# A spectral filter beside a gated MLP on one core: one complex edge column, half-array blocks of four, and the forward constant loaded later

## The chip, the core and the metric

The kernel runs on one core of a Trainium2 chip. The metric is device time in microseconds for one execution. A core has TensorE (matrix products into PSUM, eight banks of 512 fp32 columns per partition), VectorE (DVE), ScalarE (ACT), GpSimd (POOL) and SyncE (SP). SP, ACT and POOL issue transfers, which run on 16 DMA engines. In the profile PE stands for TensorE's products and PEld for its weight loads.

## What is computed

For x of 2048 x 512 (bf16):

```
g = sigmoid(sum(x * gate_w, -1))
a = irfft2(rfft2(x) * (w_r + 1j*w_i))          # 2048 x 257 filter
b = (h * tanh(softplus(h))) @ w2,  h = x @ w1 + b1     # 512 -> 1792 -> 512
out = g * a + (1 - g) * b
```

Branch a is a chain of small Fourier products, branch b two dense products. They share TensorE.

## The kernel before

**Branch b.** `f_mm1` (L790) makes h for four row tiles (512 columns) and one of 14 feature tiles, four products of 512 columns to a group; there are four chunks of 14 groups. `mish` on ACT (L799) moves it from two PSUM banks into one of three activation buffers. `f_mm2` (L831) multiplies 14 feature tiles by w2 into one 512-column bank for each of 16 row tiles, in two halves of seven products; L813 is the last tile in two column halves. Two banks (4 and 5) take mm2's results in turn. For the first NBF = 8 tiles, `evict_b` (L770) stores (1 - g) b without waiting for branch a, and `sum` (L849) adds g a later. For the others, `fin` (L841, and L820 for the last tile) combines both straight from PSUM and so needs branch a's tile first.

**Branch a, forward.** `f_tr` (L517) transposes each x tile, VectorE forms sums and differences (L532), and `f_a1` (L546 to L549) makes the transform along the 512 columns with the constant FDs: bank 0, evicted (`e1`) to In1. With 256 real and 256 imaginary columns wanted for 257 frequencies, the sine column of frequency 0, which would be zero, holds frequency 256. `f_s1` (L569, L571) is the first step along the 2048 rows. It works on half the array: the contraction is 64 deep, and two tiles' products on the upper and the lower half run at the same time. Its real input is 257 columns wide, its imaginary one 255. It takes two row tiles at a time into banks 4 to 7; `e2` evicts to Y1, and a DMA for every four tiles and half (`r1w`) writes scr1 in DRAM in pieces of 257 bf16 columns, 514 bytes. Once all is written, four DMAs (`r1r`) read it back rearranged into In2.

**Filter.** `f_s2` (L680), the second step along the rows, also uses half the array (64 output rows to a product), two units of 256 columns at a time into banks 0 and 1. VectorE multiplies each unit by the filter twice (`wm`, L691), POOL or VectorE combine (`wz`, L697) into Zb, which has three buffers of two units. Columns 0 and 256 go a way of their own: `f_s2x` (L648) for each half of the units, four small VectorE products (`zq`), four on POOL (`zr`, `zi`, `z0r`, `z0i`), a copy `wc` (L701) into Zb's first column. `f_s2i` (L711) inverts the step, half the array again, into banks 6 and 7; `e4` (1024 columns, L446 or L447) evicts, and `r2w` writes scr2, four units to a DMA in pieces of 2 KB.

**Branch a, back.** When scr2 is complete, eight `r2r` read it; then for each of the 16 tiles `f_s1i` (L744), an eviction, `f_a1i` (L756), the gated eviction `geo` on ACT (L761), and two halves of `ga` (L764). The gate's dot products `gdot` (L591) run on VectorE after the last s1; `gcol` and `omg` make g and 1 - g.

**Order.** A planner in the file (`_Graph.schedule`, L221) orders all work when the kernel is built. It gives each task a duration and a priority, takes of the tasks that can start within 0.1 us of the earliest the one of highest priority, and writes a fixed order for each engine, with semaphore waits. It does not see the chip: if a transfer is later than L293 to L297 assume, the engine's queue waits in that order. L293 to L297 put the end of a transfer at

```
xs = max(est + t.dur + 1.0, dq_free)
dq_free = xs + t.xfer
t.done = dq_free + 0.6 + 0.4 * (est > 12.0)
```

with `t.xfer` the bytes over a rate of 300 KB per us unless another is given. TensorE's branch-a work has priority, and mm1 and mm2 fill what is free; 40 warming products on zeros (L504) are dropped once the first mm1 is placed. All loads but a few go through SP in the order of the code from L475: x tile 0, x tiles 1 to 3, w1's first piece (feature tiles 0 and 1), w1's second, x tiles 4 to 7 and so on. FDs is issued on ACT's queue at the start. The wide loads of the filter and of w2 are issued by POOL.

Of the kernel before, what the change touches and what calls it, by code (L numbers as in the profile page):

```python
# [16 lines left out]
KR = 257  # L17
# [298 lines left out]
NBF = 8  # L316
# [4 lines left out]
def _build(nc, A_x, A_w_r, A_w_i, B_x, B_w1, B_b1, B_w2, gate_w, out):  # L321
# [9 lines left out]
    G = _Graph()  # L331
    es = ExitStack()
    with es:
# [14 lines left out]
        misc = sb("misc", [128, 5632], F32)  # L348
        WT = sb("WT", [128, 2, 16, KR], BF)
# [15 lines left out]
        weff = sb("weff", [128, 2, 2, 16], F32)  # L365
        q1 = sb("q1", [128, 2, 2, 16], F32)
# [8 lines left out]
        gEO = misc[:, 2048:3072].rearrange("p (b n) -> p b n", b=2)  # L375
        Zb = miscb[:, 6144:9216].rearrange("p (b u c n) -> p b u c n", b=3, u=2, c=2)
        TT = miscb[:, 9216:11264].rearrange("p (b j n) -> p b j n", b=4, j=4)
# [99 lines left out]
        dma("ld_fd", FDs[:], d_FD[:], writes=["FD"], nbytes=128 * 1536, queue="act")  # L477
        dma("ld_b1", braw[:, :], B_b1.rearrange("(ft p) -> ft p", p=128), writes=["braw"], nbytes=3584, queue="pool")
        ld_w1(0)
        ld_w1(1)  # L480
# [22 lines left out]
        for i in range(NWARM):  # L503
            G.add(f"warm{i}", "pe", 0.213, lambda e: e.matmul(ps[:, 7, 0:256], zt[:, 0:128], zt[:, :], start=True, stop=True),  # L504
               reads=["zt"], prio=1.0).filler = True
# [5 lines left out]
        for t in range(NT):  # L511
            tbk = 3 + t if 1 <= t < 4 else 1
# [30 lines left out]
        for t in range(NT):  # L543
# [15 lines left out]
            if t % 2 == 1:  # L559
                def f_s1(e, t0=t - 1):  # L560
                    ins = None
                    for tt_ in range(2):
                        tk = t0 + tt_
                        for c in range(2):
                            for bx in range(2):
                                r = slice(64 * bx, 64 * bx + 64)
                                o = ps[:, 4 + 2 * tt_ + bx, :]
                                if c == 0:
                                    ins = e.matmul(o[:, 0:KR], M1s[r, tk, 0, :], In1[r, tk, 0:KR], start=True, stop=False)  # L569
                                else:  # L570
                                    ins = e.matmul(o[:, 1:256], M1s[r, tk, 1, :], In1[r, tk, KR:512], start=False, stop=True)  # L571
                    return ins

                B47 = [("bank", i) for i in range(4, 8)]
                s1_tasks.append(pe(f"s1_{t}", 4 * mm(256) + 0.19, f_s1, reads=[("In1", t - 1), ("In1", t), ("m1", t // 8)], writes=B47, prio=SP0 + 0.4))
                yo = Y1.rearrange("p (b t) k -> p t b k", b=2)
                for i in range(2):
                    evict(f"e2_{t - 1 + i}", 514, yo[:, t - 1 + i], ps[:, 4 + 2 * i:6 + 2 * i, 0:KR],
                          [("bank", 4 + 2 * i), ("bank", 5 + 2 * i)], [("Y1", t - 1 + i)], prio=SP0 + 0.6)
            if t % 4 == 3:  # L580
                for bx in range(2):
                    b0 = 16 * bx + t - 3
                    t_r1w.append(dma(f"r1w{t}_{bx}", scr1_w[:, b0:b0 + 4, :], Y1[:, b0:b0 + 4, :],
                                     reads=[("Y1", t - i) for i in range(4)], writes=[("scr1", b0 + i) for i in range(4)],
                                     nbytes=128 * 4 * 514, prio=SP0 + 1.0))
# [3 lines left out]
        for t in range(NT):  # L589
# [3 lines left out]
                  reads=[("x", t), "gw"], writes=[("gd", t), "junk"], deps=s1_tasks[-1:])  # L593
# [9 lines left out]
        def f_wcols(e):  # L603
            ins = None
            for i in range(2):
                e.tensor_copy(out=wrv[:, i, :, 0], in_=WT[:, i, 0, 0:KR:256])
                e.tensor_copy(out=wrv[:, i, :, 1:16].rearrange("p k g -> p g k"), in_=WT[:, i, 15:0:-1, 0:KR:256])
                ins = e.tensor_scalar(out=wh[:, i, :].rearrange("p (k g) -> p g k", k=2), in0=WT[:, i, :, 0:KR:256],
                                      scalar1=0.5, scalar2=None, op0=ALU.mult)
            return ins  # L610

        G.add("wcols", "pool", 1.9, f_wcols, reads=WALL, writes=["wrv", "wh"])
        psW = ps[:, 5, 64:128]
# [7 lines left out]
        def f_weff(e):  # L621
            e.scalar_tensor_tensor(out=weff[:, 0].rearrange("p k g -> p (k g)"), in0=psW[:, 0:32], scalar=0.5, in1=wh[:, 0, :], op0=ALU.mult, op1=ALU.add)
            return e.scalar_tensor_tensor(out=weff[:, 1].rearrange("p k g -> p (k g)"), in0=psW[:, 32:64], scalar=-0.5, in1=wh[:, 1, :], op0=ALU.mult, op1=ALU.add)
# [5 lines left out]
        for hf in range(2):  # L629
            for h in range(2):  # L630
# [3 lines left out]
                                 deps=s1_tasks[-1:], nbytes=128 * 8 * 514, prio=SP0 + 1.0))  # L634
# [6 lines left out]
        for hf in range(2):  # L641
            gs = slice(8 * hf, 8 * hf + 8)

            def f_s2x(e, hf=hf):
                ins = None
                for c in range(2):
                    for h in range(2):
                        ins = e.matmul(ps[64 * h:64 * h + 64, 6, 16 * c:16 * c + 16].rearrange("p (k g) -> p k g", k=2), RF[:, c, :],  # L648
                                       In2[:, 16 * h + 8 * hf:16 * h + 8 * hf + 8, 0:KR:256].rearrange("p g k -> p k g"),
                                       start=True, stop=True)  # L650
                return ins

            s2_tasks.append(pe(f"s2x{hf}", 0.15, f_s2x, reads=[("In2", 16 * h + 8 * hf + i) for h in range(2) for i in range(8)] + ["sm"],
                               writes=[("bank", 6)]))
            xps = ps[:, 6, 0:32].rearrange("p (c k g) -> p c k g", c=2, k=2)

            def f_q(e, gs=gs, xps=xps):
                ins = None
                for c in range(2):
                    e.tensor_tensor(out=q1[:, c, :, gs], in0=xps[:, c], in1=weff[:, c, :, gs], op=ALU.mult)  # L660
                    ins = e.tensor_tensor(out=q2[:, c, :, gs], in0=xps[:, c], in1=weff[:, 1 - c, :, gs], op=ALU.mult)
                return ins

            G.add(f"zq{hf}", "dve", 0.6, f_q, reads=[("bank", 6), "weff"], writes=[("q", hf)])
            G.add(f"zr{hf}", "pool", 0.15, lambda e, gs=gs: e.tensor_tensor(out=zr[:, :, gs], in0=q1[:, 0, :, gs], in1=q1[:, 1, :, gs], op=ALU.subtract),
                  reads=[("q", hf)], writes=[("zr", hf)])
            G.add(f"zi{hf}", "pool", 0.15, lambda e, gs=gs: e.tensor_tensor(out=zi[:, :, gs], in0=q2[:, 0, :, gs], in1=q2[:, 1, :, gs], op=ALU.add),
                  reads=[("q", hf)], writes=[("zi", hf)])
            G.add(f"z0r{hf}", "pool", 0.15, lambda e, gs=gs: e.tensor_tensor(out=z0[:, 0, gs], in0=zr[:, 0, gs], in1=zi[:, 1, gs], op=ALU.subtract),
                  reads=[("zr", hf), ("zi", hf)], writes=[("z0r", hf)])  # L670
            G.add(f"z0i{hf}", "pool", 0.15, lambda e, gs=gs: e.tensor_tensor(out=z0[:, 1, gs], in0=zi[:, 0, gs], in1=zr[:, 1, gs], op=ALU.add),
# [289 lines left out]
```

## Time and profile before

| | |
|---|---|
| median of 3 runs | 144.88 us (144.8 to 145.26) |
| profiled execution | 145.94 us, span 143.9 us |
| TensorE busy | 136.0 us, 95% of the span |
| VectorE / ACT / POOL busy | 85.2 / 82.4 / 34.3 us |
| L790 (mm1), 224 products | 52.1 us busy for the 215 recorded |
| L831 (mm2), 210 products | 47.7 us busy for the 202 recorded |
| granted TensorE clock | 1.0 throughout |

A busy product of 512 columns has 379 ns in the list of groups because products overlap; in a row without gaps they follow each other every 213 ns (256 columns: 107 ns). The span runs from the first to the last instruction. The first L790 starts at 8.11 us, the last s1 at 41.61, the first s2 at 54.77, the last s2i at 92.49, the first s1i at 102.85, and the last a1i ends at 125.66; from there to 140.8 TensorE has only mm2 to do.

### The profile page before, as it was taken

The page shows a single profiled execution, that of the slowest core. Times are in us where ns is not written, and L with a number is a line of the kernel's source. Part 1 is how long each engine was busy: PE and PEld are TensorE (multiplying, and loading weights), DVE is VectorE, ACT ScalarE, POOL GpSimd, SP SyncE. Part 2 cuts the span into 40 slices and gives each one's busy share as a digit, 9 for nine tenths or more (in the row PEclk, how much of TensorE's full clock was granted, in tenths as well). Part 3 has the DMA queues.
Part 4 walks back from the last instruction along what each step waited for, and adds up shares of the span by engine and source line. Part 5 has one row for each costly group of instructions (what it writes and reads, how often), then busy time and mean ns, then how long its engine had stood idle before and what let it go on. Part 6 is the DMA issues. An engine that isn't in the chain of part 4 may idle for free.

```text
span 143.9 us, 2505 instructions
## 1 busy us (share of the span) xinstructions
PE 136.0 (95%) x928; PEld 72.4 (50%) x945; DVE 85.2 (59%) x188; ACT 82.4 (57%) x126; POOL 34.3 (24%) x69
## 2 busy tenths in 40 slices
PE   6879999999999997999999999999999999999991
PEld 4636556555544324344443544443567666644470
DVE  0256777843349996778755866500169999844141
ACT  4437998877775673791448666557557765610000
POOL 4000370030000004346418431200044365420000
PEclk9999999999999999999999999999999999999999
DMA  4899999999975396700303003035953333202032
GB/s 130 288 375 387 383 241 222 227 331 324 147 86 150 64 258 268 280 14 0 146 5 146 2 5 146 0 146 171 271 145 73 75 91 81 52 0 55 18 91 57
DMA packets 16556, 21.40 MB, mean 149 GB/s; under 512 B 1248, under 2 KB 12384, under 8 KB 16160
## 3 DMA queue, kind: packets, MB, share of 16 engines
q1 hardware_dynamic: 15408, 17.03, 42.0%
q0 software_dynamic: 832, 3.94, 10.4%
q10 hardware_dynamic: 304, 0.26, 0.8%
q8 instruction: 7, 0.11, 0.3%
q14 instruction: 5, 0.04, 0.1%
HBM read 14.93 MB, written 6.30 MB: 148 GB/s over the span
## 4 chain that ended last, share of the span: by engine, by line
PE 84%; DMA 10%; DVE 2%; issue 1%; SPq 1%
PE ps L831 30%; PE ps L790 27%; PE ps L756 5%; DMA Abuf<-scr 4%; DMA scr<-Ybuf 3%; PE ps L680 3%; PE ps L711 3%; PE ps L517 3%; PE ps L744 2%; PE ps L549 2%; PE ps L813 2%; DMA xo<-in_A_x_dram 2%; PE ps L569 2%; PE ps L571 1%; PE ps L546 1%
## 5 line engine op out<-in xcount | busy, mean ns | idle before, releaser
L790 PE MATMUL ps<-xT,w_sb 128*128 128x512 bf16 x215 | 52.1, 379 | 1.9 <-DVE yb L532 1.1
L799 ACT ACTIVATE act<-ps,b1f 128x512 bf16<-128x512 f32 x56 | 38.4, 687 | 17.6 <-PE ps L790 17.2
L831 PE MATMUL ps<-w_sb,act 128*128 128x512 bf16 x202 | 47.7, 379 | 0.4
L790 PEld LDWEIGHTS ps<-xT,w_sb 128*128 128x128 bf16 x224 | 19.9, 98 | 24.5 <-ACT act L799 4.4
L831 PEld LDWEIGHTS ps<-w_sb,act 128*128 128x128 bf16 x210 | 20.0, 98 | 22.4 <-issue 0.4
L691 DVE TENSOR_TENSOR misc<-ps,WT 128x512 f32<-128x512 f32 x32 | 19.9, 682 | 9.4 <-PE ps L680 9.4
L764 POOL TENSOR_TENSOR Tg<-misc 128x256 bf16<-128x256 f32 x14 | 11.1, 810 | 25.0 <-ACT misc L761 25.0
L697 POOL TENSOR_TENSOR misc<-misc 128x255 bf16<-128x255 f32 x19 | 13.4, 729 | 14.1 <-DVE misc L691 14.1
L447 ACT ACTIVATE Ybuf<-ps 128x514 bf16<-128x514 f32 (+1 forms) x16 | 12.5, 784 | 4.6 <-PE ps L711 4.3
L761 ACT ACTIVATE misc<-ps,gcol 128x512 f32<-128x512 f32 x16 | 10.6, 687 | 7.1 <-PE ps L756 7.1
L446 DVE CAST misc<-ps 128x512 bf16<-128x512 f32 x8 | 5.5, 681 | 13.4 <-PE ps L744 13.4
L764 DVE TENSOR_TENSOR Tg<-misc 128x256 bf16<-128x256 f32 x18 | 12.8, 747 | 0.4 <-ACT misc L761 0.4
L770 ACT ACTIVATE xo<-ps,omg 128x512 bf16<-128x512 f32 x8 | 5.5, 687 | 10.7 <-PE ps L831 7.1
L591 DVE SCALAR_TENSOR_TENSOR junk<-xo,gwb 128x512 bf16<-128x512 bf16 x16 | 11.0, 690 | 0.7
L841 DVE SCALAR_TENSOR_TENSOR xo<-ps,omg,Tg 128x512 bf16<-128x512 f32 x7 | 5.1, 745 | 7.9 <-PE ps L831 7.9
L756 PE MATMUL ps<-GDs,misc 128*128 128x256 bf16 x64 | 9.4, 273 | 0.0
L446 DVE COPY xT<-ps 128x512 bf16<-128x512 bf16 x9 | 3.8, 424 | 9.3 <-PE ps L517 9.2
L446 DVE CAST Abuf<-ps 128x512 bf16<-128x512 f32 x6 | 4.1, 690 | 7.1 <-PE ps L549 7.1
L446 DVE CAST Ybuf<-ps 128x514 bf16<-128x514 f32 (+1 forms) x8 | 6.1, 756 | 2.9 <-PE ps L571 2.9
L756 PEld LDWEIGHTS ps<-GDs,misc 128*128 128x128 bf16 x64 | 6.0, 98 | 2.3
L517 PE MATMUL ps<-pid,xo 128*128 128x128 bf16 x64 | 6.1, 225 | 0.2 <-DMA xo<-in_A_x_dram 0.2
L680 PE MATMUL ps<-Abuf,sm 128*64 128x256 bf16 x64 | 5.1, 278 | 1.2 <-DMA Abuf<-scr 1.1
(69 smaller groups left out, 123.9 us busy)
## 6 DMA issues: line engine op xcount, KB each, us to landing
scr<-Ybuf SPq DMA_DIRECT2D x8, 257.0 KB, 11.0
Abuf<-scr SPq DMA_DIRECT2D x4, 514.0 KB, 6.3
scr<-Ybuf SPq DMA_DIRECT2D x4, 512.0 KB, 3.0
Abuf<-scr SPq DMA_DIRECT2D x8, 256.0 KB, 5.3
w_sb<-in_B_w_dram POOLq DMA_DIRECT2D x2, 896.0 KB, 16.0
out_dram<-xo SPq DMA_DIRECT2D x14, 128.0 KB, 2.3
w_sb<-in_B_w_dram SPq DMA_DIRECT2D x3, 512.0 KB, 9.1
xo<-in_A_x_dram SPq DMA_DIRECT2D x3, 512.0 KB, 9.7
```

Of the source, the lines that this page charges most:

```text
L446: G.add_multi(name, [("dve", dve_dur(n), lambda e: e.tensor_copy(out=dst, in_=src)), ("act", act_dur(n), lambda e: e.activation(dst, src, ...
L447: ("act", act_dur(n), lambda e: e.activation(dst, src, AF.Copy))],
L517: ins = e.transpose(psb[:, tbk, 128 * dt_:128 * (dt_ + 1)], xo[:, t, 128 * dt_:128 * (dt_ + 1)], perm[:, :])
L591: lambda e, t=t: e.scalar_tensor_tensor(out=junk[:, :], in0=xo[:, t, :], scalar=1.0, in1=gwb[:, :], op0=ALU.mult, op1=ALU.mult, accum_out= ...
L691: lambda e, Pb=Pb, Wu=Wu, u=u, pb=pb: e.tensor_tensor(out=Pb[:, pb, :].rearrange("p (c r q) -> p c r q", c=2, r=4), in0=ps[:, u % 2, :].re ...
L697: fz = (lambda e, c=c, Pb=Pb, op=op, pb=pb, zb=zb: e.tensor_tensor(out=Zb[:, zb, pb, c, 1:256], in0=Pb[:, pb, 1:256], in1=Pb[:, pb, 257:51 ...
L756: ins = e.matmul(ps[:, yk, 256 * (j // 2):256 * (j // 2) + 256], TT[:, ts_, j, :], GDs[:, j, :], start=(j % 2 == 0), stop=(j % 2 == 1))
L761: lambda e, t=t, gb=gb, yk=yk: e.activation(gEO[:, gb, :], ps[:, yk, :], AF.Copy, scale=gcol[:, t:t + 1]),
L764: fg = (lambda e, i=i, op=op, t=t, gb=gb: e.tensor_tensor(out=ga[:, t, 256 * i:256 * i + 256], in0=gEO[:, gb, 0:256], in1=gEO[:, gb, 256:5 ...
L790: ins = e.matmul(ps[:, bank, :], w1_sb[:, dt_, 128 * ft:128 * (ft + 1)], xT[:, dt_, 4 * c:4 * c + 4, :], start=(dt_ == 0), stop=(dt_ == 3))
L799: lambda e, ft=ft, bank=bank, hb=hb: e.activation(act[:, hb, ft, :], ps[:, bank, :], AF.Mish, bias=b1f[:, ft:ft + 1]),
L831: ins = e.matmul(ps[:, bank, :], act[:, hb, ft, 128 * tl:128 * (tl + 1)], w2_sb[:, ft, :], start=(ft == 0), stop=(ft == NFT - 1))
```

## The change

1. `KR` becomes 256. Columns 0 and 256 travel as one complex column through s1, scr1, In2 and s2; s1 has 256 columns in both of its products, scr1 pieces are 512 bytes. (The filter keeps 257 columns, `KW`.) To part the two columns after s2, the spectrum at the mirrored row index is needed: a new `f_rr` on POOL makes reversed copies RR of the s2 constant, `f_s2x` (now once, twelve small products, in bank 0 after unit 0's wm) yields the column and its mirror, `rs` and `f_x0` on VectorE separate them, and `f_q` moves to POOL. The factors 0.5 in `wcols` and `weff` become 0.25.
2. s1 takes four row tiles to a block (16 products, banks 2 to 5), evicted by four `e2` of 512 columns.
3. s2 and s2i take four units to a block (16 products each); both use banks 0 to 3. Zb has two buffers of four units. Each block ends with two `e4` and one `r2w`.
4. The load of FDs moves from ACT's queue to SP's, behind w1's first piece.
5. `gdot` may start after the third of the four s1 blocks. NBF is 12.
6. Banks: mm1 6 and 7, a1i 2 and 3, the last mm2 tile's halves 2 and 3, transposes 2 to 4 for tiles 1 to 3, warming products bank 6. gEO and TT lie over P1b and Zb.

```
-KR = 257
+KW = 257
+KR = 256
-NBF = 8
+NBF = 12
...
-        gEO = misc[:, 2048:3072].rearrange("p (b n) -> p b n", b=2)
-        Zb = miscb[:, 6144:9216].rearrange("p (b u c n) -> p b u c n", b=3, u=2, c=2)
-        TT = miscb[:, 9216:11264].rearrange("p (b j n) -> p b j n", b=4, j=4)
+        gEO = misc[:, 0:1024].rearrange("p (b n) -> p b n", b=2)
+        Zb = miscb[:, 4096:8192].rearrange("p (b u c n) -> p b u c n", b=2, u=4, c=2)
+        TT = miscb[:, 4096:6144].rearrange("p (b j n) -> p b j n", b=4, j=4)
...
-        dma("ld_fd", FDs[:], d_FD[:], writes=["FD"], nbytes=128 * 1536, queue="act")
         dma("ld_b1", braw[:, :], ..., queue="pool")
         ld_w1(0)
+        dma("ld_fd", FDs[:], d_FD[:], writes=["FD"], nbytes=128 * 1536)
         ld_w1(1)
...
-            tbk = 3 + t if 1 <= t < 4 else 1
+            tbk = 1 + t if 1 <= t < 4 else 1
...
-            if t % 2 == 1:
-                def f_s1(e, t0=t - 1):
+            if t % 4 == 3:
+                def f_s1(e, t0=t - 3):
                     ins = None
-                    for tt_ in range(2):
+                    for tt_ in range(4):
                         tk = t0 + tt_
                         for c in range(2):
                             for bx in range(2):
                                 r = slice(64 * bx, 64 * bx + 64)
-                                o = ps[:, 4 + 2 * tt_ + bx, :]
-                                if c == 0:
-                                    ins = e.matmul(o[:, 0:KR], M1s[r, tk, 0, :], In1[r, tk, 0:KR], start=True, stop=False)
-                                else:
-                                    ins = e.matmul(o[:, 1:256], M1s[r, tk, 1, :], In1[r, tk, KR:512], start=False, stop=True)
+                                ins = e.matmul(ps[:, 2 + 2 * (tt_ // 2) + bx, 256 * (tt_ % 2):256 * (tt_ % 2) + 256], M1s[r, tk, c, :],
+                                               In1[r, tk, 256 * c:256 * c + 256], start=(c == 0), stop=(c == 1))
...
+                for bx in range(2):
+                    for i in range(2):
+                        b0 = 16 * bx + t - 3 + 2 * i
+                        evict(f"e2_{b0}", 512, Y1[:, b0:b0 + 2, :].rearrange("p b k -> p (b k)"), ps[:, 2 + 2 * i + bx, :],
+                              [("bank", 2 + 2 * i + bx)], [("Y1", b0), ("Y1", b0 + 1)], prio=SP0 + 0.6)
...
-                  reads=[("x", t), "gw"], writes=[("gd", t), "junk"], deps=s1_tasks[-1:])
+                  reads=[("x", t), "gw"], writes=[("gd", t), "junk"], deps=s1_tasks[2:3])
...
+        SB = (0, 1, 2, 3)
+        BSB = [("bank", i) for i in SB]
+        xps = ps[:, 0, 0:64].rearrange("p (v c g) -> p v c g", v=2, c=2)
+
+        def f_s2x(e):
+            for c in range(2):
+                for h in range(2):
+                    o = xps[64 * h:64 * h + 64, :, c, :]
+                    hr = 16 * (1 - h)
+                    e.matmul(o[:, 0, :], RF[:, c, :], In2[:, 16 * h:16 * h + 16, 0], start=True, stop=True)
+                    e.matmul(o[:, 1, 1:16], RR[:, 0, c, :], In2[:, hr + 15:hr:-1, 0], start=True, stop=True)
+                    ins = e.matmul(o[:, 1, 0:1], RR[:, 1 - h, c, :], In2[:, 16 * h:16 * h + 1, 0], start=True, stop=True)
...
+        for n in range(4):
+            u0 = 4 * n
+            zb = n % 2
+            def f_s2(e, u0=u0):
+                for i in range(4):
+                    for c in range(2):
+                        for h in range(2):
+                            ins = e.matmul(ps[64 * h:64 * h + 64, SB[i], 256 * c:256 * c + 256], RF[:, c, :], In2[:, 16 * h + u0 + i, :], ...)
...
+                if u == 0:
+                    s2_tasks.append(pe("s2x", 0.6, f_s2x, reads=[("In2", j) for j in range(32)] + ["sm", "rr"], writes=[("bank", 0)]))
...
+            pe(f"s2i_{u0}", 8 * mm(256) + 0.19, f_s2i, reads=[("Z", zb, 4)] + [("Z", zb, i, c) for c in range(2) for i in range(4)] + ["sm"],
+               writes=BSB)
+            for i in range(2):
+                v = 2 * n + i
+                evict(f"e4_{v}", 1024, T2s[:, :, 2 * v:2 * v + 2, :].rearrange("p h g k -> p h (g k)"), ps[:, 2 * i:2 * i + 2, :], ...)
...
-            yk = 6 + t % 2
+            yk = 2 + t % 2
...
-                bank = 2 + (mm1_idx % 2)
+                bank = 6 + (mm1_idx % 2)
...
-                        cs_, bk = slice(256 * i, 256 * i + 256), 5 - i
+                        cs_, bk = slice(256 * i, 256 * i + 256), 2 + i
```

## The prediction

> **What bounds the kernel now.** I read the page's busy shares first, then the chain that ended last, then the waits of TensorE, then the chain and the timelines around the half-array blocks.
>
> ```profile
> PE 136.0 (95%) x928; PEld 72.4 (50%) x945; DVE 85.2 (59%) x188; ACT 82.4 (57%) x126; POOL 34.3 (24%) x69
> ...
> PE 84%; DMA 10%; DVE 2%; issue 1%; SPq 1%
> ...
> PE ps L680 <- DMA Abuf<-scr: 1.1, 1, 1.1
> PE ps L790 <- DVE yb L532: 1.1, 1, 1.1
> PE ps L790 <- issue: 0.5, 3, 0.2
> ...
> 43.39 4.84 DMA scr<-Ybuf
> ...
> 48.70 5.94 DMA Abuf<-scr
> 54.64 0.14 issue
> 54.77 0.63 PE ps L680 x8
> ...
> 59.99 0.63 PE L680 MATMUL ps<-Abuf,sm 128*64 128x256 bf16 x8
> 60.55 0.61 PE L711 MATMUL ps<-misc,sm 64*128 64x256 bf16 x8
> 61.10 1.90 PE L790 MATMUL ps<-xT,w_sb 128*128 128x512 bf16 x8
> ...
> 40.65 1.03 PE L790 MATMUL ps<-xT,w_sb 128*128 128x512 bf16 x4
> 41.61 0.28 PE L569 MATMUL ps<-Abuf,m1g 64*128 64x257 bf16 x2
> ...
> 42.16 1.04 PE L790 MATMUL ps<-xT,w_sb 128*128 128x512 bf16 x4
> ...
> L691 DVE TENSOR_TENSOR misc<-ps,WT 128x512 f32<-128x512 f32 x32 | 19.9, 682 | 9.4 <-PE ps L680 9.4
> ```
>
> In the chain's and timeline's rows the first two numbers are start and length in us; the busy row gives each engine's total. TensorE runs without a stop from its first L790 product at 8.11 us to 140.8, but for 1.07 us before L680 and three gaps of 0.16. So the time falls only where TensorE starts sooner, has less to do, or loses the 1.07; a spectral step that gets slower costs nothing until TensorE runs out of matmuls to put beside it. The page row of L691 (columns: busy, mean ns, idle before) shows VectorE waiting 9.4 us for L680: that loop has slack too.
>
> The sum is made against the profiled execution (span 143.9 us, 145.94 in all). The median of the runs shown is 144.88, so I subtract the changes from 144.88.
>
> **Part 1, the forward constant.** Landings (issue plus time to landing): x tile 0 at 3.8, FDs at 3.6, x tiles 1 to 3 at 5.45, w1's first piece at 1.73 + 6.2 = 7.93, and the first L790 starts at 8.11. The wait list names VectorE's yb, but the product does not read yb; its last input is w1's piece. FDs' 192 KB now travel after that piece. From 5 to 10 us the transfers run at 353 GB/s, so the piece lands 192/353 = 0.54 us sooner, and the x tiles too (their evictions ended at 7.06). Next in line are w1's second piece (9.4) and x tiles 4 to 7 (10.66). TensorE would then want the second piece at about 9.8 and the x tiles at 10.6, so hardly anything of it is taken back. FDs lands near 7.9, wanted at about 9.3. SP gets one more issue of about 0.5 us, which moves the later issues on a queue whose transfers are already full (share 1.0 from 5 us). Value -0.5; ends 0 (the loads behind bind at once) and -0.65.
>
> **Part 2, s1 in blocks of four tiles.** From the timeline: four L790 products of 213 ns from 40.65 end at 41.50, L569 starts at 41.61 (0.11 to enter), and L790 is back at 42.16, 0.55 later, where four pairs of 256 columns at 107 ns take 0.43 (0.12 to leave). One excursion costs 0.23. Eight become four: -0.92. The one column less is 64 x 0.4 ns: nothing. The tiles behind an s1 block used to find 0.86 us of L790 and the s1 block as cover between two a1; three steps of four now put two L790 groups there (the steps were 1.74 and 2.17 us in turn), so the last s1 comes some 2 us later, with L790 done in the meantime: no TensorE time. Its four evictions, two per engine at 0.6 pitch, end 0.6 later. The gate products (16 x 0.74 on VectorE) move to after the third block, where VectorE works 1.4 us of 4; they may hold up an e1 by 0.7, again covered by L790.
>
> **Part 3, s2 and s2i in blocks of four units.** Now: seven adjacent pairs (59.99 to 61.10, that is 1.11 - 0.85 + 0.10 to enter = 0.36 each), a lone first s2 with s2x (0.42 over its products), a lone s2x (75.84 to 76.02, 0.30 with entry) and a lone last s2i (0.45 with its gap): 3.7 us. After: s2 and s2i share banks 0 to 3 and can no longer be adjacent: eight lone blocks x 0.23 = 1.84, and one s2x of twelve small matmuls. Four took 0.18 (45 ns each), so 0.54 + 0.12 = 0.66. Sum 2.5: -1.2 (ends -1.5 if s2x lies against an s2 block, -0.8 if it costs twice that). The Trainium skill, TensorEngine Tiling (Instruction Overhead), gives about 60 cycles for however short a matmul, an estimate of 25 ns; twelve would be 0.30, and the sum 0.24 us lower. The trace's 45 ns decides.
>
> **Part 4, the 1.07 us before L680.** TensorE's queue reached s2 before In2 was there. Lines 293 to 297 put the last write to scr1 at 3.75 us after its issue; it took 4.84. The difference is the gap. The same half megabyte in 2 KB pieces (r2w, 94.2) landed in 3.0. The new write has 512-byte pieces in place of 514: between 4.84 (gap stays, 0) and 3.0 (gap gone, -1.07). I take -0.5, halfway: in piece size it is nearest to its own row, but that row's pieces also straddled the 512-byte grid. The skill's page DMA: Bandwidth & Descriptors (Specifications) speaks against a gain: it has full rate from 512 bytes up, so that 514 would be as good; by it this term is 0 and the forecast 142.6. The row does not bear the page out: 514-byte pieces ran at 244 GB/s from 45 to 46 us, with the transfer share at 1.0, 2 KB pieces at 420.
>
> **Part 5, the closed loop.** In one four-unit block: s2 (1.1), VectorE's eight wm (4 in 2.48, so 5.0) and two or three wz (0.37 pitch), with the remaining wz on POOL at 0.70 pitch beside them: 6.0; s2i 1.1; two e4 side by side (ACT 1.02, VectorE 1.21): 1.2; five handovers of 0.1: 9.9 us a block, against 8.9 for two of today's pairs (4.45 each). s2x's chain (five small VectorE steps at 0.085 pitch, six on POOL near 0.2) ends some 3 us before the first s2i needs it. s2 starts near 55.4 (later s1, faster write), so s1i starts at 55.4 + 3 x 9.9 + 9.9 + 8.7 (today's 94.16 to 102.85) = 103.7, against 102.85. Covered by products: with twelve tiles evicted ahead of ga, their matmuls are free to run before it. New waits of TensorE at the eight handovers: today's comparable gaps are 0.16, three in sixteen; I take +0.3, ends 0 and +1.5 (eight of 0.19).
>
> **Part 6, what lies beside.** Four more tiles go through L770 (0.69 on ACT) and L849 (0.41) in place of L841 (0.75): ACT +2.7, VectorE -1.3, both under TensorE. Bank renumbering, f_rr on POOL (idle then): 0. The last tile's banks: L813 waited for nothing: 0. If the cover goes, ACT's 2.7 counts.
>
> Sum: -0.5 - 0.92 - 1.2 - 0.5 + 0.3 = -2.8, so 142.1 us. Ends: -0.65 - 0.92 - 1.5 - 1.07 = -4.1 (140.8), and 0 - 0.92 - 0.8 + 0 + 1.5 = -0.2 (144.7).
>
> **Rivals.** *A: the closed loop becomes the bound (slower).* Place: banks 0 to 3. For it: the next s2 waits for both e4, and each handover may find TensorE inside a 1.49 us half of an L831 group and ACT behind a 0.69 mish. Against: 9.4 us of waiting in today's loop were already of this kind and cost nothing. The last tiles: ga comes 24.8 us after s1i starts (127.6 - 102.85), but L831 of tiles 14 and 15 needs banks freed by ga of tile 12: s1i + 20.4 + 0.8 + 6.0. That meets the forecast's end (138.0) at s1i = 110.8, a block of 11.7 us. It costs more than the gain (145.3) from s1i = 114, a block of 12.5. With both handovers at 1.5, e4 one after the other on ACT and a mish before it: 9.9 + 3.0 + 1.5 = 14.4, s1i near 121, the end 10 us past the forecast's; halfway there, 147.
>
> *B: fewer switches, as many gaps (same).* TensorE's queue is in order; waits of 0.3 us at each of nine handovers, with neither the start nor the 1.07 gained, give -0.92 - 1.2 + 2.7 = +0.6, and half of these 144.5 to 145.3. For it: each block has one producer and one consumer in turn. Against: today's sixteen blocks show only three gaps.
>
> *C: the transfers give nothing.* Parts 1 and 4 at 0 with the switches gained: 143.1 to 144.3.
>
> **How the numbers follow.** Forecast (140.8 to 143.1) 0.58, C 0.21, B 0.07, A 0.14. The runs spread by 0.3%, which is what a measurement of this kernel can tell from no change: 144.45 to 145.3. Forecast and C lie below: 0.79 faster; B 0.07; A 0.14 slower. The range runs from 140.5, a little beyond the lower end since the write could also move s1i up, to 145.3, leaving out A and the tail of the forecast; the forecast with C alone is 140.8 to 144.3.
>
> **What would show it.** Right: first L790 near 7.6; L569's line in four blocks of 0.98; s2 and s2i in eight; the wait before s2 under 0.6; the last write to scr1 below 4.8; blocks of wm about 10 us apart; TensorE's end near 138. Wrong: gaps over 0.3 before s2 or s2i, s1i after 111, VectorE's fins waiting for ga at the end, or the first L790 still near 8.1 because w1's piece does not move.

## The result, and the profile after

| | before | after |
|---|---|---|
| median | 144.91 us (144.8 to 145.26) | 142.51 us (142.36 to 142.56) |
| ratio, 95% interval | | 0.9829 (0.981 to 0.9847) |
| profiled execution / span | 145.94 / 143.9 us | 142.56 / 140.8 us |
| first mm1 product | 8.11 | 7.26 |
| idle before the first s2 | 1.07 | 0 |
| first s1i / end of the last a1i | 102.85 / 125.66 | 108.80 / 131.61 |
| end of TensorE's products | 140.8 | 137.7 |

The time fell by 2.4 us against a forecast of 2.8. On another chip, beside the third group of experiments, the same two kernels took 145.55 and 142.30 us, ratio 0.9778 (0.9757 to 0.9799): the gain differs between chips, 2.4 and 3.25 us. Lines of the kernel after: mm1 L810, mish L819, mm2 L851 (L833 in the last tile), s1 L572, s2 L689, s2i L732, s1i L764, a1i L776.

The page of the kernel after: busy time, the chain's shares, two groups (busy, mean ns, idle before).

```profile
PE 136.2 (97%) x946; PEld 74.2 (53%) x946; DVE 86.3 (61%) x192; ACT 81.4 (58%) x128; POOL 31.9 (23%) x62
...
PE 92%; ACT 4%; DVE 0%; issue 0%
...
L810 PE MATMUL ps<-xT,w_sb 128*128 128x512 bf16 x224 | 54.2, 380 | 0.4 <-ACT act L819 0.3
...
L699 DVE TENSOR_TENSOR misc<-ps,WT 128x512 f32<-128x512 f32 x32 | 19.9, 685 | 12.6 <-PE ps L689 12.6
```

The DMA share of the chain (10% before) is gone. In its place stand 4% of ACT, which were not there. Here all 224 records of mm1 are present; before there were 215. VectorE's wait for s2 grew from 9.4 to 12.6 us, and cost TensorE nothing.

The account of TensorE from its first product to its last, taken from the starts of successive matmuls, each counted at its columns (512 in 213 ns, half that for half-array pairs) and a missing record as a product: first product -0.85; time lost in and around half-array blocks 5.0 to 3.1, -1.9; the gap before s2 -1.1; all else +0.75, the new gaps of the forward stage shown below. Together -3.1, which is the change of the span. That is 0.7 more than the change of the medians: the execution profiled before took 145.94 us, 1.0 above the median here.

The chain of the kernel after in the forward stage (start, length) shows the new gaps:

```profile
14.83 1.00 PE ps L572 x16
...
15.86 1.57 ACT Ybuf L452 x3
17.43 0.49 ACT Abuf L452
17.92 0.49 ACT xT L452
18.41 0.58 ACT act L819
...
19.04 1.04 PE ps L810 x4
...
24.43 1.57 ACT Ybuf L452 x3
...
26.98 0.58 ACT act L819
...
27.61 1.04 PE ps L810 x4
```

An s1 block frees its four banks through `e2`. Three of the four evictions stand on ACT in a row; an `e1`, an xT eviction and only then the mish that mm1's next group waits for follow. TensorE loses 0.22 us after 18.8, 0.11 after 20.1, 0.16 after 20.5, 0.45 after 27.0 and 0.09 after 29.5.

The closed loop, in the timeline of the kernel after (start, length; in brackets the idle time ahead and what ended it):

```profile
65.96 1.06 PE L689 MATMUL ps<-Abuf,sm 128*64 128x256 bf16 x16
66.95 1.90 PE L810 MATMUL ps<-xT,w_sb 128*128 128x512 bf16 x8
67.06 2.48 DVE L699 TENSOR_TENSOR misc<-ps,WT 128x512 f32<-128x512 f32 x4 [1.60 <-PE ps L689]
...
72.52 0.76 DVE L705 TENSOR_TENSOR misc<-misc 128x255 bf16<-128x255 f32 x2
73.22 1.03 PE L810 MATMUL ps<-xT,w_sb 128*128 128x512 bf16 x4
74.18 1.05 PE L732 MATMUL ps<-misc,sm 64*128 64x256 bf16 x16
```

TensorE has no gap in it. But the loop does not run at the pace of its own steps: VectorE's last combination ends at 73.28, and s2i starts 0.9 us later, behind an mm1 group that stands ahead of it in TensorE's order. s2 starts at 53.91, 65.96, 76.99 and 88.36, on the mean 11.5 us apart.

### The profile page after: what moved, and what is told of

The parts are those of the page before. It is cut to its first block, busy times and chain, and to the rows that moved or that the text cites. A ratio compares the mean times of both kernels' runs of the same rounds, so it can differ in the third digit from the quotient of the medians.

```text
span 140.8 us, 2515 instructions
## 1 busy us (share of the span) xinstructions
PE 136.2 (97%) x946; PEld 74.2 (53%) x946; DVE 86.3 (61%) x192; ACT 81.4 (58%) x128; POOL 31.9 (23%) x62
## 4 chain that ended last, share of the span: by engine, by line
PE 92%; ACT 4%; DVE 0%; issue 0%
PE ps L810 33%; PE ps L851 32%; PE ps L776 5%; PE ps L509 3%; PE ps L689 3%; PE ps L572 3%; PE ps L732 3%; PE ps L764 3%; PE ps L522 2%; ACT Ybuf L452 2%; PE ps L833 2%; PE ps L554 2%; ACT act L819 1%; PE ps L551 1%; ACT Abuf L452 1%; ACT xT L452 1%
## 5 line engine op out<-in xcount | busy, mean ns | idle before, releaser
L810 PE MATMUL ps<-xT,w_sb 128*128 128x512 bf16 x224 | 54.2, 380 | 0.4 <-ACT act L819 0.3
L819 ACT ACTIVATE act<-ps,b1f 128x512 bf16<-128x512 f32 x56 | 38.1, 690 | 21.8 <-PE ps L810 16.4
L851 PE MATMUL ps<-w_sb,act 128*128 128x512 bf16 x210 | 48.3, 379 | 0.0
L810 PEld LDWEIGHTS ps<-xT,w_sb 128*128 128x128 bf16 x224 | 20.0, 98 | 24.1 <-ACT act L819 5.7
L851 PEld LDWEIGHTS ps<-w_sb,act 128*128 128x128 bf16 x210 | 20.1, 98 | 22.4 <-issue 0.4
L699 DVE TENSOR_TENSOR misc<-ps,WT 128x512 f32<-128x512 f32 x32 | 19.9, 685 | 12.6 <-PE ps L689 12.6
L705 POOL TENSOR_TENSOR misc<-misc 128x255 bf16<-128x255 f32 x16 | 11.4, 731 | 41.0 <-DVE misc L699 41.0
L784 POOL TENSOR_TENSOR Tg<-misc 128x256 bf16<-128x256 f32 x12 | 10.3, 873 | 27.9 <-ACT misc L781 27.9
L790 ACT ACTIVATE xo<-ps,omg 128x512 bf16<-128x512 f32 x11 | 7.6, 687 | 15.2 <-PE ps L851 15.0
L451 DVE CAST Ybuf<-ps 128x512 bf16<-128x512 f32 (+1 forms) x10 | 8.8, 900 | 9.3 <-PE ps L732 8.2
L781 ACT ACTIVATE misc<-ps,gcol 128x512 f32<-128x512 f32 x16 | 10.3, 685 | 5.0 <-PE ps L776 4.0
L784 DVE TENSOR_TENSOR Tg<-misc 128x256 bf16<-128x256 f32 x20 | 12.0, 629 | 0.7 <-ACT misc L781 0.7
L452 ACT ACTIVATE Ybuf<-ps 128x512 bf16<-128x512 f32 (+1 forms) x14 | 9.4, 718 | 2.6 <-PE ps L572 1.6
L776 PE MATMUL ps<-GDs,misc 128*128 128x256 bf16 x64 | 9.3, 273 | 0.0
L452 ACT ACTIVATE Abuf<-ps 128x512 bf16<-128x512 f32 x12 | 7.2, 602 | 0.0
L776 PEld LDWEIGHTS ps<-GDs,misc 128*128 128x128 bf16 x64 | 6.0, 98 | 2.3
L522 PEld LDWEIGHTS ps<-pid,xo 128*128 128x128 bf16 x64 | 5.2, 110 | 3.0 <-issue 0.4
L705 DVE TENSOR_TENSOR misc<-misc 128x255 bf16<-128x255 f32 x16 | 6.4, 441 | 0.0
```

Of the source, the lines that this page charges most:

```text
L451: G.add_multi(name, [("dve", dve_dur(n), lambda e: e.tensor_copy(out=dst, in_=src)), ("act", act_dur(n), lambda e: e.activation(dst, src, ...
L452: ("act", act_dur(n), lambda e: e.activation(dst, src, AF.Copy))],
L522: ins = e.transpose(psb[:, tbk, 128 * dt_:128 * (dt_ + 1)], xo[:, t, 128 * dt_:128 * (dt_ + 1)], perm[:, :])
L699: lambda e, Pb=Pb, Wu=Wu, bk=bk, pb=pb: e.tensor_tensor(out=Pb[:, pb, :].rearrange("p (c r q) -> p c r q", c=2, r=4), in0=ps[:, bk, :].rea ...
L705: fz = (lambda e, c=c, Pb=Pb, op=op, pb=pb, i=i, zb=zb: e.tensor_tensor(out=Zb[:, zb, i, c, 1:256], in0=Pb[:, pb, 1:256], in1=Pb[:, pb, 25 ...
L776: ins = e.matmul(ps[:, yk, 256 * (j // 2):256 * (j // 2) + 256], TT[:, ts_, j, :], GDs[:, j, :], start=(j % 2 == 0), stop=(j % 2 == 1))
```

## The experiments

Three groups of four kernels, each group on one chip beside the kernel before, whose median there was 145.52, 145.44 and 145.55 us. Ratios are to that kernel on the same chip. The changed kernel itself ran beside the third group (`ctl`).

**1. FDs back on ACT's queue**, issued where it was before.

```
         ld_x(1, 4)
+        dma("ld_fd", FDs[:], ..., queue="act")
...
         ld_w1(0)
-        dma("ld_fd", FDs[:], ...)
```

> The changed kernel (142.5 us) with FDs loaded on ACT's queue at the start again, all else as changed. Theory 1, FDs on a second queue runs ahead of the x tiles and w1's first piece and costs them more than its 0.54 us of bandwidth: w1's piece lands near 7.9 as before the change (6.13 in the changed kernel), the first L810 starts at 8.1 in place of 7.26, the time is 143.3 (+0.85). Theory 2, only the 192 KB count: the piece lands at 6.7, the x tiles' evictions (7.21) still come last, the first L810 starts at 7.3 to 7.5, the time is 142.5 to 142.8.

143.32 us, ratio 0.9859 (0.9827 to 0.989). DMA issues of this kernel (KB each, median us from issue to landing):

```profile
xo<-in_A_x_dram SPq DMA_DIRECT2D x1, 384.0 KB, 4.1
w_sb<-in_B_w_dram SPq DMA_DIRECT2D x1, 256.0 KB, 6.3
FDs<-c_fd ACTq DMA_DIRECT2D x1, 192.0 KB, 3.1
xo<-in_A_x_dram SPq DMA_DIRECT2D x1, 128.0 KB, 3.3
```

The same of the changed kernel:

```profile
xo<-in_A_x_dram SPq DMA_DIRECT2D x1, 384.0 KB, 3.9
w_sb<-in_B_w_dram SPq DMA_DIRECT2D x1, 256.0 KB, 4.4
FDs<-c_fd SPq DMA_DIRECT2D x1, 192.0 KB, 4.5
xo<-in_A_x_dram SPq DMA_DIRECT2D x1, 128.0 KB, 2.2
```

w1's first piece takes 6.3 us again in place of 4.4 and x tile 0 3.3 in place of 2.2; the first product is at 8.17, and the last one 0.90 us later than in the changed kernel. The rest of TensorE's account is unchanged. So the move is worth its 0.9 in the profile. The medians are less sharp: this ratio lies 0.003 above the changed kernel's on its first chip and 0.008 above that on the third, which is 0.4 to 1.2 us, and six executions of this kernel spread over 1.25 us (142.74 to 143.99), four of the changed kernel over 0.2.

**2. FDs on SP, ahead of w1's first piece.**

```
         ld_x(1, 4)
+        dma("ld_fd", FDs[:], ...)
...
         ld_w1(0)
-        dma("ld_fd", FDs[:], ...)
```

> The forward constant (192 KB) is loaded on SP's queue, as in the changed kernel, but ahead of w1's first piece instead of behind it. Theory 1 (what counts is that nothing is pulled ahead on a second queue: the 192 KB in the same queue cost their own bandwidth, 0.54 us, and no more): w1's piece lands about 0.54 to 0.7 us later than the 6.1 us of the changed kernel and the first product comes at 7.2 to 7.5, since the last xT eviction ended at 7.2 anyway; ratio 0.982 to 0.985. Theory 2 (the bytes ahead of the piece delay it by 1.8 us, on whichever queue they stand): the piece lands at 7.9 and the first product comes at 8.1; ratio 0.985 to 0.989.

141.98 us, ratio 0.9777 (0.9745 to 0.981): no different from the changed kernel's 0.9778 on the third chip. Its issues:

```profile
w_sb<-in_B_w_dram SPq DMA_DIRECT2D x1, 256.0 KB, 4.0
FDs<-c_fd SPq DMA_DIRECT2D x1, 192.0 KB, 3.7
xo<-in_A_x_dram SPq DMA_DIRECT2D x1, 128.0 KB, 2.1
```

The piece is issued at about 2.2 in place of 1.73 and lands at 6.2 in place of 6.1; the first product, 7.32, waits for an xT eviction on ACT, as in the changed kernel. So it is not the 192 KB ahead of the piece that cost 1.8 us, but that they came by a second queue at the start. (There FDs is issued at 0.8 us, beside x tile 0; the same early place on SP's own queue was not run, so queue and place are not parted.) The Trainium skill, DMA: Bandwidth & Descriptors (Issuing engines are not separate DMA queues), has it that another engine's queue only saves issue time; in the two runs it also made the other queue's pieces land later (x tile 0 after 3.3 us in place of 2.1, w1's first piece after 6.3 in place of 4.0). In all twelve profiles with FDs on SP the first product starts between 6.51 and 7.32; in the two with FDs on ACT's queue at 8.11 and 8.17.

**3. s1 in blocks of two tiles again** (banks 2 and 3, then 4 and 5).

```
-            if t % 4 == 3:
-                def f_s1(e, t0=t - 3):
+            if t % 2 == 1:
+                k0 = 2 + 2 * ((t // 2) % 2)
...
+                def f_s1(e, t0=t - 1, k0=k0):
...
-                    for tt_ in range(4):
+                    for tt_ in range(2):
...
```

`gdot` keeps its place three quarters through, now behind the sixth of eight blocks.

> The changed kernel with s1 in blocks of two tiles (8 products, two banks in turn, two evictions each), all else as changed. Both theories: four more excursions into the half array at 0.23 to 0.25 cost 0.95. Theory 1, the four evictions of a four-tile block hold up ACT, and with it mish and L810: the TensorE gaps between 18 and 30 us (about 0.9 in all) go, so the time is 142.6 to 142.8. Theory 2, those gaps have another cause: they stay, 143.4.

143.99 us, ratio 0.9902 (0.9881 to 0.9923). As a ratio that is theory 2's number (143.4 of 144.91 is 0.9896), but not for theory 2's reason. Four more excursions cost 0.83 us, 0.21 each, against 0.23 in the prediction. The gaps of the ACT burst are gone. But a first product at 6.67 had to wait 0.46 us for x tile 4 at 9.4, and s1i came at 110.34 (why later was not tried), with a wait of 1.13 near the end. Experiment 8 shows what that is.

**4. The evictions of the first three s1 blocks below the mish.**

```
-                              ..., [("Y1", b0), ("Y1", b0 + 1)], prio=SP0 + 0.6)
+                              ..., [("Y1", b0), ("Y1", b0 + 1)], prio=SP0 + 0.6 if t == NT - 1 else 91.0)
```

> The evictions of the first three s1 blocks (L582, out of banks 2 to 5) get a priority below the mish of the first products, so that the planner no longer sets three of them in a row on ScalarE ahead of a mish; nothing else is edited, though the planner may order other steps otherwise too. Theory 1 (the 0.75 to 0.9 us of TensorE's gaps between 18 and 30 us come from ScalarE standing in the burst of evictions while banks 6 and 7 wait for their mish): the gaps after 18.7, 20.1, 20.5, 27.0 and 29.5 us go, their sum is under 0.3, and the time falls by 0.5 to 0.9 against the changed kernel, ratio to the kernel before 0.977 to 0.980. Theory 2 (the gaps stand for a shortage of work on TensorE that only moves): as much waiting turns up elsewhere before 45 us, for the tiles of a1 or the banks of s1, and the ratio stays at 0.982 to 0.986.

141.78 us, ratio 0.9747 (0.9721 to 0.9774). The gaps between 18 and 30 us fell from 1.03 to 0.29. Of the gain, 0.53 went to two waits for loads at 8.5 and 9.5 us, since the first product (6.51) was early. So it was run once more, beside the unedited kernel:

> The kernel with the low priority of the first three blocks' evictions again, beside the changed kernel on one chip. In its first profile the gaps between 18 and 30 us fell from 1.03 to 0.29, but a first product at 6.51 had to wait for w1's second piece (0.24) and for x tile 4 (0.29) at 8.5 and 9.5 us. Theory 1 (the ScalarE burst cost real time and the loads only take back a start earlier than about 7): 0.4 to 0.8 us below the unedited kernel beside it. Theory 2 (what the burst cost is paid anyway, to the loads at the start or to the longer queue on VectorE): within 0.3 us of it.

> The changed kernel unedited, on the same chip as the three runs beside it, since the ratio of one kernel to the kernel before may differ between chips by some 0.3%. Theory 1 (the gaps behind the s1 blocks are a property of the order): its profile shows about 1.0 us of gaps between 18 and 30 us as before (0.22, 0.11, 0.16, 0.45, 0.09), ratio 0.977 to 0.984. Theory 2 (they came from that one execution): the gaps are elsewhere or under 0.5.

141.77 us (0.974, 0.972 to 0.976) against 142.30 (0.9778, 0.9757 to 0.9799): 0.53 us. The unedited kernel shows the same five gaps as in its first profile (0.23, 0.11, 0.16, 0.45, 0.09). ACT after the first block, in the timeline of the changed kernel and then of the edited one:

```profile
15.86 1.57 ACT L452 ACTIVATE Ybuf<-ps 128x512 bf16<-128x512 f32 x3 [0.52 <-PE ps L572]
...
18.25 0.73 ACT L819 ACTIVATE act<-ps,b1f 128x512 bf16<-128x512 f32 x1
...
15.51 0.60 ACT L452 ACTIVATE Ybuf<-ps 128x512 bf16<-128x512 f32 x1 [0.52 <-PE ps L572]
16.16 0.60 ACT L452 ACTIVATE Abuf<-ps 128x512 bf16<-128x512 f32 x1
16.66 0.59 ACT L452 ACTIVATE Ybuf<-ps 128x512 bf16<-128x512 f32 x1
17.14 0.69 ACT L819 ACTIVATE act<-ps,b1f 128x512 bf16<-128x512 f32 x1
```

The mish starts at 17.14, 1.6 us after the block's first eviction; in the changed kernel it started 2.4 us after it. The burst was a real cost. This kernel is the fastest of all that ran.

**5. s2 and s2i in blocks of two units**, s2 in banks 0 and 1, s2i in 2 and 3, three buffers of Z.

```
-        for n in range(4):
-            u0, zb = 4 * n, n % 2
+        for n in range(8):
+            u0, zb = 2 * n, n % 3
...
```

> The changed kernel with s2 and s2i in blocks of two units (banks 0 and 1, banks 2 and 3; Zb as three of four buffers of two units), all else as changed. Theory 1, excursions are all that counts: eight more s2/s2i blocks, mostly in adjacent pairs, cost 0.9, 143.4, though s1i comes 4 to 8 us sooner than 108.8. Theory 2, the long closed loop (s2 starts 11.0 to 12.1 us apart) already costs something at the end: with s1i sooner the time is 142.5 or below.

143.33 us, ratio 0.9859 (0.9835 to 0.9883). Half-array time rose by 1.14 us. s1i started at 98.83, 10 us earlier, and nothing came of it at the end. What the larger blocks save is excursions; the longer loop that they bring costs nothing in the changed kernel.

**6. Rows of 257 columns through scr1, 514 bytes**; In2 and Y1 get the same width, with zeros in the last column.

```
-    scr1 = nc.dram_tensor("scr1", (32, 128, KR), BF)
+    scr1 = nc.dram_tensor("scr1", (32, 128, KW), BF)
...
```

> The changed kernel with rows of 257 columns in Y1, scr1 and In2, of which one is zero and not used: r1w writes pieces of 514 bytes again, r1r reads pieces of 4112 bytes. Theory 1, the odd piece slows the transfers: the last write to scr1 takes 4.8 us from issue to landing (2.5 in the changed kernel), the reads 5 to 6 us, and as the queue has 1.2 us in hand before s2, a gap of 0.5 to 1.2 us stands before the first s2 again: 143.0 to 143.7. Theory 2, 512 and 514 bytes are alike: landing 2.5 to 3, no gap, 142.5.

143.75 us, ratio 0.9888 (0.9862 to 0.9914). The last writes took 3.5 us, the reads 6.5 (medians; 2.5 and 4.5 in the changed kernel), and TensorE waits for the reads before s2 (excess 0.96). Whether length or place did it:

**7. Rows of 512 bytes, 514 bytes apart.**

```
-    scr1 = nc.dram_tensor("scr1", (32, 128, KR), BF)
+    scr1 = nc.dram_tensor("scr1", (32, 128, KW), BF)
...
-    dma(f"r1w{t}_{bx}", scr1_w[:, b0:b0 + 4, :], ...)
+    dma(f"r1w{t}_{bx}", scr1_w[:, b0:b0 + 4, 0:256], ...)
...
-    dma(f"r1r{hf}{h}", ..., scr1_r[:, j0:j0 + 8, :], ...)
+    dma(f"r1r{hf}{h}", ..., scr1_r[:, j0:j0 + 8, 0:256], ...)
```

> The rows written to and read from scr1 keep their 256 columns (512 bytes), but lie 514 bytes apart in scr1, as 257-column rows do. With rows of 514 bytes the last writes took 3.5 us to land and the reads 5.0 to 6.8; in the changed kernel 2.5, and 3.8 to 5.2. Theory 1 (what costs is that the pieces lie across the 512-byte grid): writes land in 3.3 to 3.7 us, reads in 5.0 or more, and TensorE waits for In2 before s2 by 0.5 to 1.1 us; ratio 0.005 or more above the unedited kernel beside it. Theory 2 (the length of the piece over 512 bytes costs): writes land in 2.4 to 2.7, no wait before s2, and the time is that of the unedited kernel within 0.4 us.

143.07 us, ratio 0.9837 (0.9814 to 0.986), 0.77 above the unedited kernel beside it. DMA issues between 36 and 56 us of this kernel:

```profile
Abuf<-scr SPq DMA_DIRECT2D x4, 512.0 KB, 6.7
scr<-Ybuf SPq DMA_DIRECT2D x2, 256.0 KB, 3.6
```

The same of the changed kernel, rows 512 bytes apart:

```profile
Abuf<-scr SPq DMA_DIRECT2D x4, 512.0 KB, 4.5
scr<-Ybuf SPq DMA_DIRECT2D x2, 256.0 KB, 2.5
```

And TensorE before s2, rows 514 apart:

```profile
52.43 1.03 PE L810 MATMUL ps<-xT,w_sb 128*128 128x512 bf16 x4
54.29 1.06 PE L689 MATMUL ps<-Abuf,sm 128*64 128x256 bf16 x16 [0.83 <-DMA Abuf<-scr]
```

The number of pieces, from the pages of this kernel and of the changed one:

```profile
DMA packets 20140, 21.38 MB, mean 151 GB/s; under 512 B 1248, under 2 KB 16480, under 8 KB 19744
...
DMA packets 16556, 21.38 MB, mean 152 GB/s; under 512 B 1248, under 2 KB 12384, under 8 KB 16160
```

The writes are the same bytes in the same 1024 pieces of 512; only their place differs, and it has the whole effect that the 514-byte rows had on their landing (3.6 and 3.5 against 2.5). So where the rows start costs, and not their length; which grid counts was not tried. The bytes themselves were no slower: at a full transfer share they moved at 284 GB/s (43 to 44 us) against 282 in the changed kernel (44 to 45). The second write, issued at 42.34, moved its last byte before 45 us and landed at 46.29; in the changed kernel, issued at 42.87, it ended at 45.12 and landed at 45.47. Most of the delay thus lies behind the last byte, and its reason stays open. The Trainium skill, DMA: Bandwidth & Descriptors (How a descriptor splits into AXI transactions), has it that a piece that does not start on a multiple of 256 bytes fetches from the boundary below it, bytes that are not used. An estimate from that page is 16 beats for an aligned 512 bytes and about 20 for one that starts anywhere, a quarter more. The equal rates of the writes do not show that cost.

The reads are no such comparison. Rows 512 bytes apart join, eight to a piece of 4096 bytes; here each row is a piece, 4096 in place of 512, which is the difference of the two rows above. In experiment 6, with pieces of 4112 bytes, the first read took 3.8 us, as in the changed kernel; only the later ones took longer, the next of them issued 2.2 us before the first had landed (0.9 in the changed kernel). How much of the wait before s2 is the writes' and how much the reads' was not parted. From its first mm1 product to its end TensorE took 131.3 us in both experiments and 130.4 in the unedited kernel.

**8. How much later s1i may come.** Both `e4` of a block on VectorE, first in all four blocks, then in two.

```
-                evict(f"e4_{v}", 1024, ...)
+                G.add(f"e4_{v}", "dve", dve_dur(1024), lambda e, ...: e.tensor_copy(...), ...)
```

> Both evictions of each s2i block (L740) run on VectorE one after the other instead of one on ScalarE beside one on VectorE. Each block of the closed loop gets about 1.2 us longer (a VectorE eviction of 1024 columns takes 1.21), and s1i starts near 113.6 in place of 108.8; the matmuls are the same. Theory 1 (rival A's point in the prediction: the end follows s1i once it starts after 110.8): the end moves by about 2.8 us, ratio 0.999 to 1.005, and TensorE shows waits for ga through the banks of its last tiles. Theory 2 (the tail has more reserve than that point says, as the last ScalarE and VectorE steps run beside products): time unchanged within 0.5 us, ratio 0.980 to 0.986. In between, the end moves by the part of 4.8 us that the reserve does not take.

146.83 us, ratio 1.0099 (1.0073 to 1.0124): slower than the kernel before. s1i starts at 112.99, 4.7 us later counted from the first product; TensorE has 3.6 us of waits after 127, all for evictions of the inverse steps, and 0.7 us more than in the changed kernel follow its last product.

> Both evictions of an s2i block on VectorE in the first two of the four blocks only. With all four, s1i came 4.7 us later and the end 3.7 later, so that about 1.1 us of reserve is left in the tail, and not the 2 us that rival A's point (110.8) left. Theory 1 (reserve 1.1 us): s1i 1.9 to 2.5 us later than in the changed kernel, and the end 0.8 to 1.4 us later, ratio 0.006 to 0.010 above the unedited kernel beside it, with waits of TensorE for L451's or L452's evictions of the inverse steps. Theory 2 (rival A's point as stated): the end within 0.4 us of the unedited kernel. Theory 3 (every delay of s1i counts in full): 1.9 to 2.5 us later.

143.62 us, ratio 0.9868 (0.985 to 0.9887), 1.32 above the unedited kernel beside it. s1i came 1.58 us later (110.30 against 108.72; 2.0 counted from the first product, 0.3 of it a wait for x tile 4), and nearly all of that was lost: more than theory 1's reserve of 1.1 us allows, and nothing like theory 2's. The timelines say why. The changed kernel, TensorE:

```profile
126.23 1.67 PE L851 MATMUL ps<-w_sb,act 128*128 128x512 bf16 x7
127.74 1.04 PE L776 MATMUL ps<-GDs,misc 128*128 128x256 bf16 x8
128.61 0.61 PE L764 MATMUL ps<-m1g,Abuf 128*128 128x128 bf16 x8
129.06 1.67 PE L851 MATMUL ps<-w_sb,act 128*128 128x512 bf16 x7
130.57 1.04 PE L776 MATMUL ps<-GDs,misc 128*128 128x256 bf16 x8
```

With s1i 1.58 later (L856, L781 and L769 are the same lines there, L866 is `fin`):

```profile
127.73 1.67 PE L856 MATMUL ps<-w_sb,act 128*128 128x512 bf16 x7
129.24 1.04 PE L781 MATMUL ps<-GDs,misc 128*128 128x256 bf16 x8
130.11 0.61 PE L769 MATMUL ps<-m1g,Abuf 128*128 128x128 bf16 x8
131.68 1.05 PE L781 MATMUL ps<-GDs,misc 128*128 128x256 bf16 x8 [0.96 <-ACT misc L452]
131.87 1.53 DVE L866 SCALAR_TENSOR_TENSOR xo<-ps,omg,Tg 128x512 bf16<-128x512 f32 x2
132.90 1.46 PE L856 MATMUL ps<-w_sb,act 128*128 128x512 bf16 x6 [0.17 <-issue]
```

The inverse steps go in pairs of tiles, and while a pair is evicted TensorE does one half of an mm2 tile, seven products, 1.49 us. The changed kernel has eight such halves for eight pairs. TensorE is never idle before s1i, so whatever s1i is late by is spent on such halves; here one is gone, and the last pair stands bare: 1.13 us before its last a1i, and 0.12 after it (the 0.33 before the group at 132.90 holds a missing record, six of seven products). With all four blocks, three are gone. The products that follow the last pair, those of tiles 14 and 15, can't take the place: tile 14 writes bank 4, which is free only when `fin` of tile 12 (L866, 131.87) is done, and tile 15 writes banks 2 and 3, which a1i uses. So the reserve is a count of halves that may run before ga, and the changed kernel has none over. The same wait of 1.13 in experiment 3, with s1i at 110.34, is this.

**9. Eight tiles ahead of ga, as before.**

```
-NBF = 12
+NBF = 8
```

> Only the first eight tiles, in place of twelve, are evicted ahead of ga (the four that the change added go back to L861's form). Theory 1 (twelve tiles are what lets a later s1i cost nothing): products of the tiles from 8 on hold banks 4 and 5 until ga of their tile, so with s1i near 108 TensorE either waits for ga or does the inverse steps close together and then the products; ga of tile 8 comes near s1i + 13, six tiles of 3.0 us stand behind it, and the end moves by 3 to 6 us: ratio 1.003 to 1.024, with a wait of over 1 us on TensorE after 108. Theory 2 (the planner only puts the products elsewhere, ScalarE saves 2.7 us and the sum is as long): ratio 0.980 to 0.986.

150.28 us, ratio 1.0315 (1.0281 to 1.0348), beyond theory 1's range; in four of the six executions the granted clock was 0.989, and the two at 0.999 took 149.27 and 149.46. The profiled execution (149.27) has a span of 147.5, 6.7 more than the changed kernel. s1i stays where it was, and the inverse steps come without cover, as in this row of its timeline:

```profile
118.36 0.61 PE L764 MATMUL ps<-m1g,Abuf 128*128 128x128 bf16 x8
121.19 1.05 PE L776 MATMUL ps<-GDs,misc 128*128 128x256 bf16 x8 [2.22 <-DVE misc L451]
```

TensorE's gaps after 100 us add up to 7.2. The larger NBF is not a side of this change, it is what makes the late s1i payable.

## Why the prediction was right or wrong

The forecast, 142.1, was right in sign and nearly in size: -2.8 against -2.4 here and -3.25 on the third chip. Partly that is luck. In the profile three terms came out better than taken (part 1 by 0.35, part 4 by 0.6, part 5 by 0.3), and a cost that was put at nothing, the burst of evictions, took 0.75 of it back.

- **Part 1, -0.5 (ends 0 and -0.65).** Profile to profile it was -0.85, outside the ends. The step that failed is the price by bandwidth, 192 KB over 353 GB/s: the piece came 1.8 us sooner, not 0.54, and in experiment 2, with those bytes in front of it on its own queue, it landed only 0.1 later. What is late next was also wrong: not w1's second piece but the third xT eviction on ACT (6.61 + 0.60), at 7.2. Against the median the term is smaller than in the profile, since the execution profiled before was 1.0 us above its median; the other terms alone explain nearly all of the 2.4 on that chip. On the third chip the same two kernels lie 3.25 us apart. That the landing of the first loads differs between executions and chips is one possible reason; it was not tried.
- **Parts 2 and 3, -0.92 and -1.2.** The excursions were rightly priced: -1.9 measured for -2.1, and +0.83 and +1.14 when each is undone. s2x cost about 0.40, not 0.66: its twelve products start within 0.20 us. The 45 ns a product taken for it held the way out of the half array, which 0.12 then counted again; the estimate of 0.30 that was set aside was the nearer one. Of the 3.7 us counted before, some 0.4 were two missing records (see part 5).
- **Part 2, the four evictions.** The step that failed is "two per engine at 0.6 pitch, end 0.6 later", with no TensorE time set against it: three went to ACT, and the mish behind them held mm1's two banks. Some +0.75 us, of which 0.53 was won back in experiment 4.
- **Part 4, -0.5 (0 to -1.07).** All of it came, -1.1. The doubt that the old row's pieces also straddled the grid was right: for the writes, experiment 7 shows their place to be the cause and their length to be none. The reading that failed is the one by rate, 244 GB/s against 420: rows of 512 bytes, on the grid, move at 282 with the share at 1.00, no faster than rows 514 apart, and what they gain is the landing. With rows 514 apart the last write took 3.9 us, though, and before 4.84; the other 0.9 us were not tried.
- **Part 5.** New waits in the loop: 0 for the +0.3 taken. The step "three comparable gaps of 0.16" was an error of reading: each stands ahead of mm1 products of which the program has a multiple of four, and the trace 19, 7 and 7. One of them, in the kernel before:

```profile
84.93 1.67 PE L790 MATMUL ps<-xT,w_sb 128*128 128x512 bf16 x7 [0.16 <-issue]
```

So a record is missing there, and TensorE did not wait: the first profile of the changed kernel has every record and no such gap, its second (`ctl`) lacks 16 records and has such gaps. The block was 11.5 us, not 9.9: handovers of 0.1 left out that a step stands behind what TensorE has in front of it in its order (0.9 us in the row shown). s1i came at 108.8 instead of 103.7.

- **Part 6.** ACT did not get 2.7 us more: its busy time fell from 82.4 to 81.4, and VectorE's rose from 85.2 to 86.3. Nothing hung on it.
- **Rival A** (0.14) did not occur but was closer than its numbers said. Its point for the forecast's end was s1i at 110.8, but 110.3 already cost 1.3 us (experiment 8), and a line between the two runs there (0.9868 at 110.3 and 1.0099 at 113.0, on two chips) meets the kernel before near 111.8, not 114. Its mechanism was half right. The waits stand before an inverse step that has no mm2 half as cover; but tile 14 could not give that half because its bank is held until ga of tile 12, which is the condition that A named. **Rival B** needed waits of 0.3 at each handover, and there were none. **Rival C** had both transfers at nothing; experiments 1 and 6 show a price for both.

## What to carry to other kernels

Filler work is a stock: where a side chain gets longer beside a full engine, count the pieces of filler left at the place where the chain's end needs them, and not only the engine's idle time, which stays at zero until the last piece is gone. A block twice as large hands its consumers twice the evictions at once; look whose queue they stand in and what waits behind them. Where a group has one product too few beside a gap of about one product's length, look for a missing record before you call it a wait.

## What the runs showed that was not expected

- 192 KB on ACT's queue delayed the SP queue's pieces by far more than their bytes: x tile 0 landed after 3.3 us in place of 2.2 and w1's first piece after 6.3 in place of 4.4, while the same bytes on SP ahead of that piece left it at 4.0. Why the later piece is hit harder was not settled.
- Writes of rows of 512 bytes took 3.6 us in place of 2.5 to land when the rows lay 514 bytes apart in DRAM, with the bytes moving at the same rate (284 and 282 GB/s).
- The time outside the span is 2.0 us in the kernel before (145.94 - 143.9) and 1.8 in the kernel after; with FDs back on ACT's queue 1.9. What the difference consists of was not tried.
